# Opening loads reordered, the norm gains spread by a matmul, and three instead of five head groups transposed on TensorE

## The chip, the cores and the metric

One core of one Trainium2 chip. The time is device microseconds of a whole run of the kernel; the runs of one kernel lie 1 to 3 us apart, so a difference is read from the interval given with it. "PE" is TensorE, "PEld" its loading of weights, "ACT" ScalarE, "DVE" VectorE, "POOL" GpSimd, "SP" the queue of SyncE, which here only issues DMAs. PEclk is the granted share of the TensorE clock. A trace is one profiled run; its times count from the start of the span.

## The reference, cut to what matters

```python
# q, k, v: (8, 12, 448, 64); g_q, g_k: (64,)
q_n, k_n = rmsnorm(q, g_q), rmsnorm(k, g_k)
attn = softmax(q_n @ k_n.T / 8)          # per head
x = (attn @ v) -> (3584, 768)            # heads side by side
out = ((x @ w1) * (x @ w2)) @ w3 @ w_out # w1, w2: 768x1024; w3: 1024x1024; w_out: 1024x768
```

The kernel multiplies w3 and w_out once (w34 = w3 @ w_out) and then needs three products per token.

## The kernel before: the parts that matter here

The work is cut into 24 quads of 4 heads. Each quad has 4 slots; in slot t = 4 i + sl PE computes a quarter of quad i's scores, a part of quad i-1's P.V, and "fillers". In slots 1 to 13 the fillers are the w34 product: 8 transposes of w3 chunks and 16 product units. Quad n's normalised q and k are prepared some slots earlier and are needed transposed (qkT). For the first N_PE_T quads PE transposes them; for the others a DMA transpose, issued by SP, does it.

```python
    N_PE_T = 5
    LAG = 4
    SHIFT = [0, 0, 0, -1, -2, -3, -4]        # quad 1, 2, ...: slots earlier than PREP says
    PREP = {"load": -8, "sq0": -5, "red0": -5, "sq1": -4, "red1": -4, "alpha": -3,
            "sc0": -3, "t0": -2, "sc1": -2, "t1": -1}
    ...
        if pe:
            s["qks", pr] = qks               # prep_pe_transpose: 8 PE transposes and a DVE copy
        else:
            nc.sync.dma_start_transpose(
                out=s["qkT"][:, pr], in_=qks.rearrange("p t j h d -> p (t j h d)"))
    ...
        nc.gpsimd.dma_start(out=gq_b, in_=g_q.unsqueeze(0).broadcast_to([NP, D]))
        nc.gpsimd.dma_start(out=gk_b, in_=g_k.unsqueeze(0).broadcast_to([NP, D]))
        ...
        load_qk(0, split=2, k_eng=nc.scalar)   # q on SP, k on ACT's queue
        load_qk(1)                             # quad 2's load follows in slot 0
        nc.gpsimd.tensor_copy(out=gate, in_=st[0]["k"][:, HQ - 1, 0, 0:1])  # weights wait here
        load_wout(0, 0); load_wout(0, 1)       # half of w_out        (joined in one line here)
        for c in range(4):
            load_w3(c)
        load_v(0)
        load_wout(1, 0); load_wout(1, 1)       # the other half
        # in the slots: w3 4, 5, v 1, w3 6, 7, v 2, then 16 loads of w1/w2, then v 3
```

## Time and profile before

| | before |
|---|---|
| median of the first 3 runs | 391.38 us |
| span of the profiled run | 389.7 us |
| PE busy | 372.7 us (96%) |
| ACT, DVE busy | 285.1, 242.3 us |
| first w3 transpose on PE | 20.45 us |

PE is the bound. The row of granted clock of the page has 40 slices of 9.7 us, in tenths:

```profile
PEclk9579999999999999999999999999999999999999
```

The 5 and the 7 are the second and third slice, 9.7 to 29 us. Everything after is full speed.

### The profile page before, as it was taken

The page shows a single profiled execution, that of the slowest core. Times are in us where ns is not written, and L with a number is a line of the kernel's source. Part 1 is how long each engine was busy: PE and PEld are TensorE (multiplying, and loading weights), DVE is VectorE, ACT ScalarE, POOL GpSimd, SP SyncE. Part 2 cuts the span into 40 slices and gives each one's busy share as a digit, 9 for nine tenths or more (in the row PEclk, how much of TensorE's full clock was granted, in tenths as well). Part 3 has the DMA queues.
Part 4 walks back from the last instruction along what each step waited for, and adds up shares of the span by engine and source line. Part 5 has one row for each costly group of instructions (what it writes and reads, how often), then busy time and mean ns, then how long its engine had stood idle before and what let it go on. Part 6 is the DMA issues. An engine that isn't in the chain of part 4 may idle for free.

```text
span 389.7 us, 14802 instructions
## 1 busy us (share of the span) xinstructions
PE 372.7 (96%) x6688; PEld 193.4 (50%) x6688; DVE 242.3 (62%) x383; ACT 285.1 (73%) x467; POOL 35.3 (9%) x61
## 2 busy tenths in 40 slices
PE   5489999999999999999999999999999999999995
PEld 1154554544544455445544554445445555456563
DVE  1776766887767577567766766757776672234232
ACT  4469889998888885897899768888889857751210
POOL 5332530000000000000000000000000000000000
PEclk9579999999999999999999999999999999999999
DMA  8999998376994479575878489659855651003014
GB/s 196 221 236 239 221 229 172 64 153 142 208 200 87 113 159 226 119 161 98 188 172 155 83 210 206 84 109 212 197 87 122 121 140 26 3 12 114 2 26 140
DMA packets 78367, 55.08 MB, mean 141 GB/s; under 512 B 37824, under 2 KB 72160, under 8 KB 78304
## 3 DMA queue, kind: packets, MB, share of 16 engines
q1 hardware_dynamic: 61568, 41.30, 44.4%
q0 software_dynamic: 16256, 12.38, 22.0%
q8 instruction: 52, 0.85, 1.0%
q10 hardware_dynamic: 480, 0.46, 0.4%
q14 instruction: 11, 0.09, 0.1%
HBM read 46.72 MB, written 11.01 MB: 148 GB/s over the span
## 4 chain that ended last, share of the span: by engine, by line
PE 88%; DMA 4%; ACT 3%; DVE 2%; POOL 0%; issue 0%; ACTq 0%
PE pa L314 19%; PE po L314 19%; PE pb L314 19%; PE pv L259 15%; PE sc L235 12%; PE wps L301 4%; DMA w3s<-in_moe_w_dram 3%; DMA k_sb<-in_k_dram 1%; PE w3T_ps L293 1%; ACT P L244 1%; ACT sq L157 1%; ACT w34s L286 1%; PE qkT_ps L220 1%; DVE qtmp L188 1%; DVE qks L201 0%; POOL w_outs L140 0%
## 5 line engine op out<-in xcount | busy, mean ns | idle before, releaser
L244 ACT ACTIVATE P<-sc 112x896 bf16<-112x896 f32 x192 | 165.3, 915 | 42.1 <-PE sc L235 42.1
L344 DVE TENSOR_TENSOR abT<-pb,a_sb 128x448 bf16<-128x448 f32 x64 | 40.0, 625 | 77.1 <-PE pb L314 56.7
L314 PE MATMUL pa<-xT,w1s 128*32 128x448 bf16 x1536 | 84.0, 353 | 0.0
L314 PE MATMUL pb<-xT,w2s 128*32 128x448 bf16 x1536 | 83.8, 352 | 0.0
L314 PE MATMUL po<-w34s,abT 128*32 128x384 bf16 x1792 | 78.0, 326 | 0.0
L166 DVE TENSOR_REDUCE ssq<-sq 112x16 f32<-112x1024 f32 x48 | 58.3, 1215 | 13.9 <-ACT sq L157 13.9
L314 PEld LDWEIGHTS <-abT 128*32 128x32 bf16 x1792 | 47.4, 97 | 27.6 <-issue 2.4
L235 PE MATMUL sc<-qkT 64*112 64x448 bf16 x384 | 57.4, 378 | 0.7 <-DVE qkT L223 0.7
L314 PEld LDWEIGHTS <-w2s 128*32 128x32 bf16 x1536 | 41.2, 97 | 31.3
L314 PEld LDWEIGHTS <-w1s 128*32 128x32 bf16 x1536 | 39.8, 96 | 34.0 <-issue 4.7
L331 ACT CAST a_sb<-pa 128x448 bf16<-128x448 f32 x64 | 33.9, 530 | 26.5 <-PE pa L314 26.5
L363 DVE COPY o_sb<-po 128x384 f32<-128x384 f32 x56 | 31.2, 557 | 31.5 <-PE po L314 31.5
L259 PE MATMUL pv<-P,v_sb 112*32 112x448 bf16 x768 | 45.1, 355 | 0.0
L120 POOL DMA_DIRECT2D v_sb<-in_v_dram x24 | 17.0, 708 | 238.8 <-PE pv L259 217.6
L188 DVE TENSOR_TENSOR qtmp<-q_sb,alpha 112x512 bf16<-112x512 f32 x48 | 32.8, 683 | 6.1 <-ACT alpha L177 6.1
L235 PEld LDWEIGHTS <-qkT 64*112 64x112 bf16 x384 | 17.4, 126 | 31.8 <-issue 29.1
L201 DVE TENSOR_TENSOR qks<-k_sb,alpha 112x512 bf16<-112x512 f32 x48 | 32.9, 684 | 0.0
L157 ACT ACTIVATE sq<-q_sb 112x512 f32<-112x512 f32 x48 | 30.4, 634 | 1.6 <-DMA q_sb<-in_q_dram 1.6
L275 DVE TENSOR_TENSOR xT<-pv,r 128x448 bf16<-128x448 f32 x48 | 29.6, 617 | 3.2 <-PE pv L259 3.2
L157 ACT ACTIVATE sq<-k_sb 112x512 f32<-112x512 f32 x48 | 30.0, 625 | 0.0
L259 PEld LDWEIGHTS <-v_sb 112*32 112x32 bf16 x768 | 16.2, 95 | 23.7 <-issue 15.2
L301 PE MATMUL wps<-w_outs,w3T 128*128 128x384 bf16 x128 | 23.7, 335 | 0.0
(36 smaller groups left out, 174.4 us busy)
## 6 DMA issues: line engine op xcount, KB each, us to landing
q_sb<-in_q_dram SPq DMA_DIRECT2D x23, 448.0 KB, 5.5
k_sb<-in_k_dram SPq DMA_DIRECT2D x23, 448.0 KB, 6.1
v_sb<-in_v_dram POOLq DMA_DIRECT2D x24, 224.0 KB, 4.6
out_dram<-o_sb SPq DMA_DIRECT2D x8, 336.0 KB, 3.8
out_dram<-o_sb SPq DMA_DIRECT2D x8, 288.0 KB, 3.3
w3s<-in_moe_w_dram POOLq DMA_DIRECT2D x8, 256.0 KB, 15.1
out_dram<-o_sb SPq DMA_DIRECT2D x8, 240.0 KB, 4.3
w_outs<-in_moe_w_out_dram POOLq DMA_DIRECT2D x4, 384.0 KB, 13.4
```

The costliest lines, as they stand in the source:

```text
L157: nc.scalar.activation(out=sq[:, t], in_=src[:, hs], func=AF.Square)
L166: nc.vector.tensor_reduce(out=s["ssq"][:, :, hs, :], in_=s.pop(("sq", pr)), axis=AX, op=ADD)
L188: nc.vector.tensor_tensor(out=qtmp.transpose([0, 2, 1, 3]), in0=s["q"][:, hs], in1=alpha[:, 0, hs].unsqueeze(3).broadcast_to([NP, 2, J, D] ...
L201: nc.vector.tensor_tensor(out=qks[:, 1].transpose([0, 2, 1, 3]), in0=s["k"][:, hs], in1=alpha[:, 1, hs].unsqueeze(3).broadcast_to([NP, 2, ...
L235: nc.tensor.matmul(out=sc[:, u, 0:S], lhsT=qkT[u * D : (u + 1) * D, pr, J + jk, :], rhs=qkT[u * D : (u + 1) * D, pr, 0:J, :].rearrange("d ...
L244: nc.scalar.activation(out=P[:, 2 * pr : 2 * pr + 2, jk, :], in_=sc[:, :, 0:S], func=AF.Exp)
L259: nc.tensor.matmul(out=ps[h * HALF : (h + 1) * HALF, :], lhsT=w, rhs=P[:, h, jk, :], start=(jk == 0), stop=(jk == J - 1), tile_position=(0 ...
L301: nc.tensor.matmul(out=ps[:, 0:NH], lhsT=w3T[:, gc, fc * 128 : (fc + 1) * 128], rhs=w_outs[:, gc, nh * NH : (nh + 1) * NH], start=(gc == 0 ...
L314: nc.tensor.matmul(out=ps[32 * h : 32 * h + 32, 0:n], lhsT=lhsT[:, 32 * h : 32 * h + 32], rhs=rhs, start=start, stop=stop, tile_position=( ...
L331: nc.scalar.copy(out=a_sb, in_=ps[:, 0:S])
L344: nc.vector.tensor_tensor(out=abT[bp][:, fi, odd * S : (odd + 1) * S], in0=ps[:, 0:S], in1=a_tiles.pop((b, fi)), op=MULT,)
L363: nc.vector.tensor_copy(out=o_sb[:, nh * NH : (nh + 1) * NH], in_=ps[:, 0:NH])
```

## The change

Its intent: get w3's chunks to PE sooner (they gate the w34 product), get the weights going sooner, take the two gains off the weight queue, and take transposes off PE.

```diff
-    N_PE_T = 5
+    N_PE_T = 3
-    LAG = 4
+    LAG = 8
+    LOADS_0 = ["o0", "w0", "w1", "w2", "v0", "w3", "w4"]   # o: half of w_out, w: w3 chunk
+    LOADS_1 = ["w5", "v1", "w6", "w7", "o1", "v2"]
+    GATE = ("q", 0)
...
-        nc.gpsimd.dma_start(out=gq_b, in_=g_q.unsqueeze(0).broadcast_to([NP, D]))
-        nc.gpsimd.dma_start(out=gk_b, in_=g_k.unsqueeze(0).broadcast_to([NP, D]))
+        nc.scalar.dma_start(out=g_row[:, 0], in_=g_q.unsqueeze(0))
+        nc.scalar.dma_start(out=g_row[:, 1], in_=g_k.unsqueeze(0))
...
-        nc.gpsimd.tensor_copy(out=gate, in_=st[0]["k"][:, HQ - 1, 0, 0:1])
+        nc.gpsimd.tensor_copy(out=gate, in_=st[0][GATE[0]][:, GATE[1], 0, 0:1])
...
-                nc.vector.tensor_tensor(out=gq_b, in0=gq_b, in1=gk_b, op=MULT)
-                nc.vector.tensor_scalar(out=g_b, in0=gq_b, scalar1=8.0, ..., op0=MULT)
+                nc.vector.scalar_tensor_tensor(out=gp_row, in0=g_row[:, 0], scalar=8.0,
+                                               in1=g_row[:, 1], op0=MULT, op1=MULT)
+                nc.tensor.matmul(out=g_ps, lhsT=ones_row, rhs=gp_row, start=True, stop=True)
+                nc.vector.tensor_copy(out=g_b, in_=g_ps)
```

LAG = 8 puts all the product units that need the second half of w_out behind those that need the first.

More of the change, by code (lines that the diff above doesn't have):

```diff
@@ L59 @@
     big_pool = ctx.enter_context(tc.tile_pool(name="big", bufs=2))
-    N_PE_T = 5
+    N_PE_T = 3
     N_SQ_ACT = 24
     W34_EV = "DA"
-    LAG = 4
+    LAG = 8
+    LOADS_0 = ["o0", "w0", "w1", "w2", "v0", "w3", "w4"]
+    LOADS_1 = ["w5", "v1", "w6", "w7", "o1", "v2"]
+    GATE = ("q", 0)
+    QK1_AT = -1
     SHIFT = [0, 0, 0, -1, -2, -3, -4]
@@ L81 @@
     w3T = big_pool.tile([128, CF, DFF], BF, tag="big", name="w3T")
-    gq_b = const.tile([NP, D], FP, name="gq_b")
-    gk_b = const.tile([NP, D], FP, name="gk_b")
+    g_row = const.tile([1, 2, D], FP, name="g_row")
+    gp_row = const.tile([1, D], BF, name="gp_row")
+    ones_row = const.tile([1, NP], BF, name="ones_row")
     g_b = const.tile([NP, D], BF, name="g_b")
@@ L145, in load_wout, with load_any @@
         )
+    def load_any(x):
+        kind, a = x[0], int(x[1])
+        if kind == "o":
+            load_wout(a, 0)
+            load_wout(a, 1)
+        elif kind == "w":
+            load_w3(a)
+        else:
+            load_v(a)
     def prep_sq(i, pr, on_act=False):
@@ L405 @@
         nc.vector.memset(ones, 1.0)
+        nc.vector.memset(ones_row, 1.0)
         load_qk(0, split=2, k_eng=nc.scalar)
+        nc.scalar.dma_start(out=g_row[:, 0], in_=g_q.unsqueeze(0))
+        nc.scalar.dma_start(out=g_row[:, 1], in_=g_k.unsqueeze(0))
         nc.scalar.preload_act_table_set("natural_log_exp_and_others")
-        load_qk(1)
+        if QK1_AT < 0:
+            load_qk(1)
         make_identity(nc, ident)
-        nc.gpsimd.tensor_copy(out=gate, in_=st[0]["k"][:, HQ - 1, 0, 0:1])
-        load_wout(0, 0)
-        load_wout(0, 1)
-        for c in range(4):
-            load_w3(c)
-        load_v(0)
-        load_wout(1, 0)
-        load_wout(1, 1)
+        nc.gpsimd.tensor_copy(out=gate, in_=st[0][GATE[0]][:, GATE[1], 0, 0:1])
+        for x in LOADS_0:
+            load_any(x)
         warm(16)
@@ L423 @@
             if pr == 0:
-                nc.vector.tensor_tensor(out=gq_b, in0=gq_b, in1=gk_b, op=MULT)
-                nc.vector.tensor_scalar(
-                    out=g_b, in0=gq_b, scalar1=8.0, scalar2=None, op0=MULT
-                )
+                nc.vector.scalar_tensor_tensor(
+                    out=gp_row, in0=g_row[:, 0], scalar=8.0, in1=g_row[:, 1],
+                    op0=MULT, op1=MULT,
+                )
+                g_ps = mm_psum.tile([NP, D], FP, tag="mm", name="g_ps")
+                nc.tensor.matmul(
+                    out=g_ps, lhsT=ones_row, rhs=gp_row, start=True, stop=True
+                )
+                nc.vector.tensor_copy(out=g_b, in_=g_ps)
             prep_scale(0, pr, pe=True)
@@ L430 @@
                 prep_pe_transpose(0, 0)
-        wq = [lambda c=c: load_w3(c) for c in range(4, CF)]
-        wq.insert(2, lambda: load_v(1))
-        wq.append(lambda: load_v(2))
+        wq = [lambda x=x: load_any(x) for x in LOADS_1]
         for h in range(HQ):
@@ L475 @@
                 t = 4 * i + sl
+                if t == QK1_AT:
+                    load_qk(1)
                 mine = agenda.pop(t, [])
```

## The prediction

> **What bounds the kernel now.** I read the busy table per stretch first, then the chain that ended last, then the timeline and transfers of the opening. The table, cut at three borders (columns: stretch, length, busy time and instruction count of PE, PEld, DVE, ACT, POOL, then granted clock, DMA share, GB/s):
>
> ```profile
> 0.00:25.00 25.00, 13.95 (x66) 6.43 (x67) 11.60 (x20) 11.40 (x21) 10.31 (x22) 0.73 1.06 217
> 25.00:68.00 43.00, 41.71 (x427) 22.78 (x425) 30.79 (x49) 38.73 (x67) 13.10 (x22) 1.00 1.11 217
> 68.00:385.00 317.00, 317.00 (x6200) 164.18 (x6196) 199.38 (x315) 234.93 (x381) 11.93 (x17) 1.00 0.59 125
> ```
>
> From 68 us to 385 us PE has no gap, and the diff touches nothing there but a few early transposes. So the end moves by as much as PE's progress at 68 us moves. All that can be won lies in 0 to 25 us (11 us of idle PE, and a mean clock of 0.73) and in the 1.3 us of gaps from 25 to 68 us. The chain in order of time (start us, length us, what) says what holds the opening:
>
> ```profile
> 1.19 5.17 DMA k_sb<-in_k_dram
> 6.36 0.05 issue
> 6.42 0.18 POOL gate L410
> 6.60 1.48 POOL w_outs L140 x2
> 8.07 12.33 DMA w3s<-in_moe_w_dram
> 20.41 0.05 issue
> 20.45 1.05 PE w3T_ps L293 x8
> ```
>
> The first chunk of w3 lands at 20.41 us, PE's first w3 transpose starts at 20.45 us, and from there PE hardly stops. That landing is the bound of the opening. The 2.9 us which VectorE loses to the two gains are not on this path:
>
> ```profile
> 10.15 0.22 DVE L424 TENSOR_TENSOR gq_b<-gq_b,gk_b 112x64 f32<-112x64 f32 x1 [3.10 <-DMA gk_b<-in_g_k_dram]
> 10.52 0.68 DVE L188 TENSOR_TENSOR qtmp<-q_sb,alpha 112x512 bf16<-112x512 f32 x1
> 16.00 0.31 SPq L109 DMA_DIRECT2D q_sb<-in_q_dram  x1
> ```
>
> In the first line VectorE sits idle 3.10 us for g_k. Its next useful work, the scaling at 10.52 us, could have begun at 7.63 us, where alpha ends. The third line is the q load of quad 3, which waits until quad 0's scaling has freed its buffer.
>
> The transfers: q/k of quads 0 to 2 fill queue 1 first. The DMA view of 5 to 12 us, then of 19 to 27 us (queue: packets, MB, share):
>
> ```profile
> q1 hardware_dynamic: 1512, 1.49, 85.7%
> q0 software_dynamic: 64, 0.06, 16.9%
> ...
> q0 software_dynamic: 1010, 1.04, 75.9%
> q1 hardware_dynamic: 907, 0.91, 40.5%
> ```
>
> The weights (queue 0) are issued from 6.54 us, but until 12 us that queue moves only the 0.06 MB of the gain broadcasts; its first weight packet starts at 12.2 us. Later the two queues share by packets, nearly 1:1.
>
> **What the Trainium skill says.** "DMA: Bandwidth & Descriptors", section "Issuing engines are not separate DMA queues": transfers from any engine run on the same 16 DMA engines and interleave. The trace agrees: the DMA line reads 9 throughout from 6 us, so an earlier start of one load is a later end of another. Same page, "Queues, rings and completion order": a DMA engine goes round-robin over the queues it has work for, by packets. The 1010 to 907 packets above agree. "TensorE: Matmul & The Clock Gate", "Part 1: The HAM clock gate": idle for about 3.4 us brings half clock, as much sustained work brings it back. The trace agrees roughly: the warm-up ends at 6.45 us, the clock is 0.50 from about 11.7 us, and back at 1.00 at 25.0 us, 4.5 us after the w3 transposes began. Same page, "Part 4: PE-mode transpose": the result goes to PSUM, so a VectorE copy follows; that copy is 0.62 us here.
>
> **The change part by part.**
>
> Gains as one row. Removed: two broadcast loads (2 x 28 KB) from the weight queue, and 0.42 us of VectorE. Added: two one-row loads on ACT's queue behind k (that queue's last k lands near 6.4 us, so the row by about 7 us), one small VectorE operation, one matmul with 64 columns, and one PSUM copy, together about 0.7 us by estimate. The reduction ends at 7.04 us, so qtmp starts at about 7.8 instead of 10.52 us: quad 0 is ready 2.5 to 3 us earlier. None of that reaches the end, because PE then waits longer for w3. It has a price instead: quad 0's buffers come free at about 13.2 instead of 16.0 us, so quad 3's q and k (0.92 MB) are issued then. Their first packets followed 3 us after issue before (16.0 to 19.0 us), so they join at about 16.2 us, while w_out and w3 are still under way.
>
> Gate on the first q. That half lands at 4.62 us against 6.36 us for the last k, so the weights are issued 1.7 us earlier, and their first packet moves from 12.2 to at best 10.5 us. Queue 1 then still has 0.35 MB + 1.6 us x 0.22 MB/us = 0.70 MB left. Sharing packet by packet (768 B of w_out against 1024 B of q/k), queue 0 has moved 0.53 MB when queue 1 has drained; with 0.245 and 0.205 MB/us as the rates of each alone, that takes 2.9 + 2.6 = 5.5 us, so until 16 us. Before, queue 0 had also moved 0.53 MB by 16 us (12 to 16 us view). So the early gate buys nothing for w3: the wires were full, only the order changed.
>
> Order of the loads. The first three (w_out half, 0.79 MB; w3 chunk 0, 0.26 MB) keep their places, so nothing moves here for the first transpose. From 16.2 us queue 0 now shares with quad 3: the last 0.26 MB of w_out and the 0.26 MB of chunk 0 give away about 0.3 MB, that is some 1.2 us, against 0.3 us given away before; minus 0.2 us for the removed broadcasts. First w3 landing: **later by 0.8 us** (0 to 1.5). Moving the other half of w_out back brings w3 chunks 4 to 7 earlier by up to 5 us, but PE waited for none of those after 25 us, so it is worth nothing. LAG = 8 makes the second-half products come last, as that order needs; the counts per slot are the same.
>
> Three quads on PE instead of five. Quads 3 and 4 lose 32 PE transposes. The timeline shows what one set of 8 occupies:
>
> ```profile
> 53.93 0.56 PE L220 MATMUL qkT_ps<-ident,qks 112*128 112x112 bf16 x8
> 54.42 0.58 PE L235 MATMUL sc<-qkT 64*112 64x448 bf16 x4
> ```
>
> From start to start 0.4 to 0.5 us, so 4 sets are 1.6 us, and quad 4's sets also cost 0.6 us of waiting for qks (67.2 to 67.8 us). Saved on the path: **2.2 us**. Given back: quad 3's set 0 now travels by DMA. Its qks is done at about 52.8 us and its scores start at 58.0 us. Before, such transfers landed thus, on a half-empty DMA:
>
> ```profile
> DMA to landing us min/median/max: 2.9/4.3/6.7
> ```
>
> At 53 us the DMA is still full of w1/w2/v. A transpose is 896 packets of 256 B, 56 per engine; alternating with 2048 B weight packets of 172 ns each it would move slowly until these end, about 56 to 58 us. I expect landing at 57 to 61 us. Also, in SP's order quad 5's q and k now stand between quad 3's two transposes. They are issued near 54 us, not 41 us, and set 1 lands behind 0.92 MB at about 65 us, just when it is needed (65.3 us). Stall of PE: 0 to 3 us, **1.4 us taken**.
>
> Sum: + 0.8 (w3 later) + 0.2 (cold clock a little longer) - 2.2 + 1.4 = + 0.2 us. I shade this by 1.3 us, since the stall needs single-packet alternation, for which this trace has no example with transposes, and since the other parts are all aimed the right way: **390.3 us**.
>
> **The rivals.** (1) The weights really come earlier: if their late start is a delay of 5.6 us from issue rather than a full DMA, and quad 3's load starts late enough, chunk 0 lands 1 to 2 us sooner and the time is 387 to 388 us. For: 12.2 us follows 6.54 us with no weight packet between. Against: total bytes ahead of chunk 0 are the same. (2) The DMA transposes become the bound at slots 12 and 14: 393 to 395 us. For: a DMA at over 100% share there. Against: they are only 0.46 MB, and need about 1.2 us each when alone. (3) The clock: quad 0's earlier work could shorten or shift the cold stretch; its length can differ by a 3.4 us window, at half clock 1.7 us of work.
>
> **Range and chances.** The parts have about 1, 1 and 1.5 us of doubt, together 2 to 2.5 us: 387.3 to 393.3 us. 2% is 7.8 us; the opening would have to deliver w3 near 12 us for that, or stall twice as long as the worst I see. Faster 0.04, same 0.94, slower 0.02.
>
> **What would show it.** qtmp's first start near 7.8 us; first weight packet near 10.5 us; quad 3's q load issued near 13 us; first w3 transpose at 20.5 to 22 us; 6 copies of qkT from PSUM, not 10; and PE idle at quad 3's scores, ended by a DMA. The prediction is wrong if the first w3 transpose starts before 19.5 us, or if PE waits over 3 us for a qkT.

## The result, and the profile after

| | before | after |
|---|---|---|
| median, runs of the same rounds (4 each) | 391.58 us | 396.25 us |
| lowest to highest | 390.85 to 392.08 | 395.76 to 396.57 |
| ratio after / before | | 1.012 (95%: 1.010 to 1.0139) |

The kernel is 1.2% slower, 4.7 us: within 2%, but above the predicted range (387.3 to 393.3 us).

The table per stretch, after, with the borders of the prediction's table and one more at 100 us (columns: stretch, length, busy time and count of PE, PEld, DVE, ACT, POOL, granted clock, DMA share, GB/s):

```profile
0.00:25.00 25.00, 15.27 (x90) 7.34 (x91) 13.84 (x25) 12.92 (x23) 9.20 (x21) 0.80 1.05 225
25.00:68.00 43.00, 37.84 (x347) 19.20 (x344) 22.84 (x35) 32.89 (x59) 12.28 (x21) 0.92 1.10 200
68.00:100.00 32.00, 30.55 (x544) 14.86 (x540) 25.78 (x40) 29.94 (x51) 2.10 (x3) 1.00 0.77 146
100.00:385.00 285.00, 285.00 (x5588) 146.95 (x5584) 175.52 (x278) 209.61 (x336) 10.53 (x15) 1.00 0.67 125
```

Before 25 us PE has done more (90 matmuls, not 66) at a better clock. Between 25 and 68 us it was busy for 3.9 us less (37.84 us, not 41.71; 347 matmuls, not 427), and at a lower clock. From 100 us it is full again, as before. So the opening was a gain, and the loss lies between 25 and 75 us. The chain that ended last shows both (start us, length us, what):

```profile
4.62 0.05 issue
4.68 0.18 POOL gate L427
4.86 1.55 POOL w_outs L145 x2
6.41 11.88 DMA w3s<-in_moe_w_dram
18.29 0.05 issue
18.34 1.05 PE w3T_ps L308 x8
...
48.78 1.47 PE wps L316 x9
50.26 9.51 DMA qkT<-qks
59.76 0.04 issue
59.81 0.99 PE sc L250 x3
60.80 1.62 PE pv L274 x15
62.42 4.44 PE wps L316 x16
```

The first six lines answer to those of before: the first w3 transpose comes at 18.34 us, 2.1 us earlier. The line at 50.26 us is new: quad 3's first DMA transpose is issued then, and PE's scores wait for it until 59.8 us. The line at 62.42 us: 16 matmuls of the product (two units of 8) take 4.44 us there; 16 of them took 2.7 us before. The waits of PE in the first 100 us, largest first (total, times, longest):

```profile
PE sc L250 <- DMA qkT<-qks: 5.1, 1, 5.1
...
PE sc L250 <- ACT P L259: 1.4, 2, 1.0
```

And what SP did meanwhile, and how long its transposes took over the whole run:

```profile
50.26 1.32 SPq L225 DMA_TRANSPOSE qkT<-qks  x1
51.67 1.25 SPq L114 DMA_DIRECT2D q_sb<-in_q_dram  x1
53.02 0.68 SPq L114 DMA_DIRECT2D k_sb<-in_k_dram  x1
...
DMA to landing us min/median/max: 3.0/4.0/11.3
```

The longest before was 6.7 us. Of the loads that quad 5 needs, issued at 51.67 and 53.02 us, the kernel before had issued its q at 41.24 us; they are behind the transpose now in the order in which SP issues. (That delay turned out to cost nothing; see e5.)

### The profile page after: what moved, and what is told of

Its sections match the earlier page's. It is cut to its first block, busy times and chain, and to the rows that moved or that the text cites. A ratio compares the mean times of both kernels' runs of the same rounds, so it can differ in the third digit from the quotient of the medians.

```text
span 394.5 us, 14750 instructions
## 1 busy us (share of the span) xinstructions
PE 373.3 (95%) x6657; PEld 191.1 (48%) x6657; DVE 240.2 (61%) x380; ACT 285.3 (72%) x467; POOL 34.1 (9%) x59
## 4 chain that ended last, share of the span: by engine, by line
PE 88%; DMA 6%; ACT 3%; DVE 1%; POOL 0%; issue 0%
PE pa L329 19%; PE po L329 19%; PE pb L329 18%; PE pv L274 15%; PE sc L250 12%; PE wps L316 4%; DMA w3s<-in_moe_w_dram 3%; DMA qkT<-qks 2%; ACT P L259 1%; DMA q_sb<-in_q_dram 1%; PE w3T_ps L308 1%; ACT sq L172 1%; POOL w_outs L145 0%; ACT w34s L301 0%; DVE ssq L181 0%; PE qkT_ps L235 0%
## 5 line engine op out<-in xcount | busy, mean ns | idle before, releaser
L250 PE MATMUL sc<-qkT 64*112 64x448 bf16 x384 | 58.3, 381 | 7.3 <-DMA qkT<-qks 5.1
L316 PE MATMUL wps<-w_outs,w3T 128*128 128x384 bf16 x128 | 24.8, 346 | 0.0
```

Of the source, the lines that this page charges most:

```text
L250: nc.tensor.matmul(out=sc[:, u, 0:S], lhsT=qkT[u * D : (u + 1) * D, pr, J + jk, :], rhs=qkT[u * D : (u + 1) * D, pr, 0:J, :].rearrange("d ...
L316: nc.tensor.matmul(out=ps[:, 0:NH], lhsT=w3T[:, gc, fc * 128 : (fc + 1) * 128], rhs=w_outs[:, gc, nh * NH : (nh + 1) * NH], start=(gc == 0 ...
```

## The experiments

Every run below gave correct results. All times are medians, with the ratio to the kernel before of the same rounds; the four at the end (e13 to e16) are single runs. I give "the first w3 transpose" from each trace.

### Which part makes the loss: e1, e2, e8

The changed kernel with quads 3 and 4 back on PE:

```diff
-    N_PE_T = 3
+    N_PE_T = 5
```

> The changed kernel with quads 3 and 4 transposed on PE again. Theory 1 (the late DMA transpose of quad 3 and the half clock behind it are the whole loss, the opening is a gain): first w3 transpose near 18.3 us as in the changed kernel, no PE wait for a DMA at slot 12, time 389.3 us (388.5 to 390.2). Rival (the earlier opening is lost again later by itself, e.g. ACT or w1/w2 become the bound): 391 us or more.

Measured: 390.36 us, ratio 0.9955 (0.9931 to 0.998). No PE wait after 25 us up to 60 us. So everything else in the change is a gain of 1.8 us (0.0045 x 391.7), a little less than I expected: the median is 0.2 us outside my range.

The kernel before with only the transposes changed (N_PE_T = 5 to 3):

> The kernel before with quads 3 and 4 transposed by DMA, nothing else. Theory 1: PE waits 4 to 6 us for quad 3's first transpose, the clock falls to half, time 396 to 399 us. Rival (the stall comes from the new order of the loads, which puts the weight traffic on top of the transpose): PE waits under 2 us, time 390 to 392.5 us.

Measured: 399.24 us, ratio 1.0185 (1.0157 to 1.0213). PE waits 5.0 us for the transpose, and the clock falls behind it:

```profile
PE sc L235 <- DMA qkT<-qks: 5.0, 1, 5.0
...
62.00:69.00 7.00, 6.71 (x35) 2.81 (x36) 0.00 (x0) 3.33 (x5) 0.00 (x0) 0.54 0.85 159
```

The rival (the new order of the loads makes the stall) is out: the stall is there with the old order.

The changed kernel with only quad 4 and later on the DMA transpose (N_PE_T = 3 to 4):

> The changed kernel with only quad 4 (not 3) on the DMA transpose. Theory 1 (only quad 3's transposes meet the full DMA): no PE wait for a DMA, and 1.4 us of PE time saved against five quads on PE: 388.6 to 390 us. Rival (any transpose before the weights are done stalls PE): 392 us or more.

Measured: 389.17 us, ratio 0.994 (0.9915 to 0.9965). Quad 3 alone costs 1.012 - 0.994, 1.8% or 7.1 us. The cause sits in one quad. That quad 4 on the DMA is a gain is not shown: e8 and e1 differ by 1.2 us between the medians, but their intervals overlap, and the traces place the difference in the opening (first w3 transpose at 17.89 us in e8, 19.54 in e1). From quad 3's first scores to the first product with w1, the stretch that holds quad 4's transposes, PE needs 10.56 us in e1 (56.89 to 67.45) and 10.51 us in e8 (54.98 to 65.49). Without the transposes PE waits there for ACT's exponentials, 1.4 us in two waits, as it does in the changed kernel.

### Why quad 3's transpose costs more than its wait: e5

Dummy matmuls where PE would stand still:

```diff
+                if t == 12:
+                    warm(20)
                 if i < NQ:
                     qk_exp(i, sl)
```

> The changed kernel with 20 dummy matmuls on PE just ahead of quad 3's scores, where PE waits for the DMA transpose (about 4.3 us of work inside a 5.1 us wait; their result is not used). Theory 1a (the wait costs twice: its own 5 us, and about 3 us because PE comes out of it at half clock for 6 us): the wait for the transpose still ends near 59.8 us, the clock stays 1.00, time 392.5 to 394.2 us. Rival (the half clock is hidden behind other waits): 395.7 to 397 us.

Measured: 393.71 us, ratio 1.0058 (1.0029 to 1.0087). The scores still started at 59.7 us, and quad 5's q was issued at 51.45 us, as late as in the changed kernel. The stretch of the stall and the one behind it, in the changed kernel:

```profile
54.70:59.80 5.10, 0.01 (x1) 0.00 (x0) 1.22 (x1) 1.77 (x4) 0.00 (x0) 0.93 1.32 186
59.80:67.00 7.20, 7.19 (x38) 2.97 (x40) 0.00 (x0) 3.44 (x6) 0.00 (x0) 0.58 0.81 163
```

and with the dummies:

```profile
54.70:59.80 5.10, 4.20 (x21) 1.77 (x21) 1.22 (x1) 1.54 (x4) 0.00 (x0) 1.00 1.34 187
59.80:67.00 7.20, 7.20 (x68) 3.28 (x68) 2.07 (x4) 5.95 (x11) 0.00 (x0) 1.00 0.77 161
```

Behind the stall PE was equally busy in both, but at clock 0.58 it got through 38 matmuls, at 1.00 through 68. The dummies compute nothing that is used, and give back 1.012 - 1.0058, that is 2.4 us. The first product with w1, in the changed kernel, with the dummies, and in e8:

```profile
73.20 1.32 PE L329 MATMUL pa<-xT,w1s 128*32 128x448 bf16 x24
70.21 1.32 PE L329 MATMUL pa<-xT,w1s 128*32 128x448 bf16 x24
65.49 1.32 PE L329 MATMUL pa<-xT,w1s 128*32 128x448 bf16 x24
```

Counted from quad 3's first scores (59.81, 59.70, 54.98 us) that is 13.39, 10.51 and 10.51 us. So with the clock kept up nothing is left of the loss behind the stall; in particular the late loads of quad 5 cost nothing. The wait is paid twice: 5.1 us of standing, and 2.4 us (by the ratios) to 2.9 us (by these traces) of coming out cold, that is at half clock.

### Why the transpose is slow: e6, e7

The changed kernel with v of quad 3 and later held back until quad 3's scores are out, so that the weight queue is empty sooner:

```diff
-        wq.append(lambda: load_v(3))
...
+                if t == 12:
+                    nc.gpsimd.tensor_copy(out=gate, in_=st[3]["P"][:, 0, 0, 0:1])
+                    load_v(3)
```

> The changed kernel with the loads of v for quad 3 and later held until quad 3's first scores are out (a POOL copy of one column of P ahead of them). Theory 1b (quad 3's transpose is slow because its 256 B packets alternate with the weight queue's packets): its second half no longer meets v packets and takes 0.6 instead of 2.3 us; it lands near 58 us, not 59.8; the wait falls to about 3.3 us; time 391.5 to 394.5 us, the lower end if the shorter wait no longer drops the clock. Rival (the transpose is slow by itself or by its issue): lands at 59.5 us or later, time 396 us.

Measured: 392.68 us, ratio 1.0019 (0.9994 to 1.0043). The wait fell to 2.3 us, more than I had expected. The transpose's packets took from 54.5 to 57.0 us; in the changed kernel from 54.2 to 59.1 us. It met little other traffic (139 packets of the weight queue from 54 to 57 us), but the clock fell all the same:

```profile
59.80:67.00 7.20, 7.20 (x56) 3.26 (x57) 2.47 (x5) 4.77 (x11) 1.97 (x3) 0.84 0.95 134
```

The third number from the end is the clock, 0.84 (0.58 in the changed kernel). Cut finer, PE resumed at 57.67 us at full clock, 1.00 until 58.7 us, and then had 0.50 from 58.75 to 62.1 us; in the changed kernel it has 0.50 from 59.1 to 65.8 us. What the two queues carried in the changed kernel from 54 to 59 us:

```profile
DMA packets 1966, 0.92 MB, mean 184 GB/s; under 512 B 961, under 2 KB 1868, under 8 KB 1966
q0 software_dynamic: 997, 0.64, 87.2%
q1 hardware_dynamic: 969, 0.28, 43.6%
```

The transpose is 896 packets of 256 B on q1. In these 5 us it got about one packet for each of the weight queue's, 969 to 997. By the first line, what it met was mostly packets of 512 B to under 2 KB (907; v's rows are 512 B), and only 98 larger ones.

The second test of the same theory was a cure that failed: prepare quads 3 and 4 two slots earlier (and quads 5 and 6 one).

```diff
-    SHIFT = [0, 0, 0, -1, -2, -3, -4]
+    SHIFT = [0, 0, -2, -3, -3, -4, -4]
```

> The changed kernel with the preparation of quads 3 and 4 moved two slots earlier (of quads 5 and 6 one or none), so that quad 3's transposes are issued near 40 us. Theory 1 (the lead of two slots is too short while the weights are being loaded): no PE wait for a DMA, the clock stays 1.00 after 25 us, time 387.5 to 389.5 us. Rival (the transposes stop something else, or ACT and VectorE pay for the earlier preparation): 391 us or more.

Measured: 396.75 us (394.19 to 400.46; the longest was a slow run and is not in the ratio), ratio 1.0107 (1.0073 to 1.0141). My expectation was wrong. The transpose was issued at 45.6 us, into denser weight traffic. From 49 to 58 us the queues carried:

```profile
q0 software_dynamic: 959, 1.45, 94.2%
q1 hardware_dynamic: 915, 0.23, 21.9%
```

Again nearly one to one, but the weight queue's packets are larger (1.45 MB in 959, against 0.64 MB in 997), so the same 896 small packets took 8.4 us. In e8, where quad 4's transpose meets no weights (63 to 65 us):

```profile
q1 hardware_dynamic: 951, 0.25, 74.3%
```

it took 1.3 us. So 1.3, 2.5, 4.9 and 8.4 us of packets for the same transfer, in the order of the traffic beside it. That this traffic makes the transpose slow is shown by e6 and e8; that the two queues alternate by packets is an explanation that fits the counts. It doesn't cover all of the delay: from issue to first packet the transpose took 3.9 us in the changed kernel (50.26 to 54.17 us), 3.6 us in e6, 4.0 us in e7, but 1.3 us in e8 (62.01 to 63.26 us). Until 54.1 us queue 1 moved nothing in the changed kernel, and the weight queue was full. What holds the start back stays open. And in e7 the delay had another victim: DVE stood 4.4 us because its buffer was still being read by the transpose.

```profile
59.59 0.42 DVE L210 TENSOR_TENSOR qks<-qtmp,g_b 112x512 bf16<-112x512 bf16 x1 [4.37 <-DMA qkT<-qks]
```

More lead does not help when the lead reaches back into denser traffic; fewer transposes under that traffic do (e8).

### Where the opening's gain comes from: e3, e4, e10

The gains as one row, nothing else:

> The kernel before with only the gains as one row (matmul spread). Theory A (the two broadcast loads slow the shared DMA engines and put some of them behind): w3 chunk 0 lands 1 to 2 us earlier (18.5 to 19.5 us), time 389.5 to 390.6 us. Rival B (the earlier gate is what brings w3 forward; VectorE was never on the path): w3 chunk 0 stays at 20 to 20.5 us, time 391 to 392 us.

Measured: 391.23 us, ratio 0.9985 (0.996 to 1.001). The first w3 transpose came at 17.95 us, 2.5 us earlier, but the time did not follow. With the gate on the first q added:

> The kernel before with the one-row gains and the gate on the first q. Theory A (bytes are conserved, the gate only reorders): within 0.4 us of the run with the one-row gains alone. Rival B (gate): 1 to 2 us faster than that run, first w3 transpose near 18.3 us, time 389 to 389.8 us.

Measured: 391.47 us, ratio 0.9998 (0.997 to 1.0025). The first w3 transpose at 18.24 us, and no gain at all. The trace says where it went, from 25 to 40 us:

```profile
PE w3T_ps L294 <- DMA w3s<-in_moe_w_dram: 2.0, 1, 2.0
```

(L294 is the w3 transpose in that kernel.) PE, 2.2 us ahead, ran into the chunk of w3 that stands behind the second half of w_out in the old order, at 31.4 us, and stood there for 2.0 us. (In e3 it was 1.0 us.) Only the new order:

```diff
-        for c in range(4):
-            load_w3(c)
-        load_v(0)
-        load_wout(1, 0)
-        load_wout(1, 1)
+        # w3 0, 1, 2, v 0, w3 3, 4; later w3 5, v 1, w3 6, 7, both parts of w_out, v 2
-    LAG = 4
+    LAG = 8
```

> The kernel before with only the new order of the loads and LAG = 8. Theory (chunk 0 keeps its place, so w3's first transpose stays near 20.4 us; the order pays only once chunk 0 is early and chunk 3 becomes the next wait): 391 to 391.8 us. Rival (the order alone gives the opening's gain): 390.3 us or less.

Measured: 390.83 us, ratio 0.9972 (0.9946 to 0.9997): first w3 transpose at 20.48 us as before, and yet some 1.1 us faster, between my two expectations. It has no PE wait between 25 and 60 us. The kernel before had one there, and I had read it wrongly:

```profile
34.21 0.62 PE L293 MATMUL w3T_ps<-ident,w3s 128*128 128x128 bf16 x8 [0.62 <-ACT sq L157]
34.21 0.45 PEld L293 LDWEIGHTS <-w3s 128*128 128x128 bf16 x8 [1.06 <-DMA w3s<-in_moe_w_dram]
```

The first line puts PE's 0.62 us down to ACT's squares, which w3's transpose does not read. The trace's landing records have chunk 4 of w3 at 34.17 us, and the weight load on PE (PEld) at the same 34.21 us is put down to a w3 load. It was the DMA. So the order removes a wait that exists before, and a larger one that the other two parts would create. The intervals of e1, e3, e4 and e10 overlap one another, so the times alone don't rank these parts; as one opening (e1) they are 1.8 us.

### What moves the first chunk: e9, e13 to e16

Is it the removed broadcasts, or the side effect that two more loads on the hardware queues delay quad 2's q and k from 2.71 to 5.0 us? The gains' rows from POOL's queue:

```diff
-        nc.scalar.dma_start(out=g_row[:, 0], in_=g_q.unsqueeze(0))   # and g_k
+        nc.gpsimd.dma_start(out=g_row[:, 0], in_=g_q.unsqueeze(0))   # and g_k
```

> The kernel before with the gains as one row each, but loaded from POOL's queue, where the broadcasts were, so that quad 2's q and k are issued as early as before (2.7 us). Theory A (the broadcast packets of up to 1.5 us themselves hold up the DMA engines and leave them uneven): w3 chunk 0 lands at 18 to 19 us as with the rows on ACT's queue. Rival (it is the later issue of quad 2's q and k, 5.0 us in place of 2.7, that lets the weights through): chunk 0 at 20 us or later. Time 390.5 to 391.8 us either way.

Measured: 391.23 us, ratio 0.9983 (0.9952 to 1.0014), first w3 transpose at 19.49 us: between the two. The opposite test, broadcasts kept and two unused one-row loads on ACT's queue:

> The kernel before, broadcasts kept, with two extra one-row loads on ACT's queue behind k into a tile that nothing reads. Theory L (the two loads on a hardware queue delay quad 2's q and k to 5.0 us and that lets the weights through): quad 2's q is issued near 5 us and the first w3 transpose starts at 18 to 19 us. Theory A (the broadcasts hold the engines up): quad 2's q is issued near 5 us, yet the first w3 transpose stays at 20 to 20.6 us. 19.2 to 19.8 us: both, about half each.

> The one-row gains from POOL's queue once more (first look: 19.49 us). Theory A: the first w3 transpose at 18 to 19 us. Theory L: at 20 us or later. Both parts: 19.2 to 19.8 us again.

> The one-row gains on ACT's queue once more, for the spread: the first w3 transpose at 17.9 to 19.2 us (first look 17.95 us).

> The kernel before once more, for the spread of its first w3 transpose: 20.3 to 20.7 us (first look 20.45 us; two other kernels with the broadcasts 20.55 and 20.48 us).

Measured, first w3 transpose: e13 20.11 us (quad 2's q was issued at 5.04 us, as meant; one run, 391.60 us), e14 19.53 us (391.32 us), e15 19.55 us (391.26 us), e16 19.62 us (391.23 us). e13 is what theory A says, e14 repeats e9. The plain repeats e15 and e16 both missed what I expected of them: the same kernel's first w3 transpose moves by 0.8 us (before: 20.45 and 19.62) and 1.6 us (gains' rows: 17.95 and 19.55) from trace to trace. Taken together:

| kernels | traces | first w3 transpose, mean (lowest to highest) |
|---|---|---|
| broadcasts, gate on k (before, e2, e10, e13, e16) | 5 | 20.24 us (19.62 to 20.55) |
| one-row gains, gate on k (e3, e9, e14, e15) | 4 | 19.13 us (17.95 to 19.55) |
| one-row gains, gate on the first q (after, e1, e4 to e8, e12) | 8 | 18.51 us (17.89 to 19.54) |

The later issue of quad 2 does not do it by itself (e13). The one-row gains bring about 1.1 us, the gate about 0.6 us; with this spread neither share is more than a tendency, their sum, 1.7 us, is clear of it. The mechanism behind the 1.1 us is not shown: the broadcast packets last up to 1.6 us in the first trace, which fits.

### Can the opening go further: e11, e12

The best version so far (four quads on PE) with two load buffers instead of three, so that quad 2's q and k come behind the first weights:

```diff
-    load_pool = ctx.enter_context(tc.tile_pool(name="load", bufs=3))
+    load_pool = ctx.enter_context(tc.tile_pool(name="load", bufs=2))
```

> The changed kernel with four quads on PE and two, not three, load buffers for q and k, so that quad 2's q and k (0.92 MB) are issued only when quad 0's buffers are free, near 14 us, behind w_out and w3's first chunks. Theory (chunk 0 waits for the bytes ahead of it): chunk 0 lands 1.5 to 3 us earlier, near 16 us, and the time falls to 386.8 to 388.6 us. Rival (the later loads of every quad then stall the squares on ACT): 389.5 us or more, with ACT waiting for q.

Measured: 391.97 us, ratio 1.0005 (0.998 to 1.0031). The opening did as expected: first w3 transpose at 16.17 us. The rival took it back later, from 20 to 110 us:

```profile
ACT sq L172 <- DMA k_sb<-in_k_dram: 2.0, 2, 1.9
```

ACT waits for a late k, PE for ACT, and from 60 to 70 us the clock has a mean of 0.83.

Four quads on PE with 16 dummy matmuls in the idle stretches of the opening:

```diff
+                warm_mm(5)          # behind the gains' copy
...
                 if t == 0:
+                    warm_mm(6)
                     prep_pe_transpose(0, 1)
+                if t == 1:
+                    warm_mm(5)
```

> The changed kernel with four quads on PE and 16 dummy matmuls in PE's idle stretches of the opening (5 after the gain matmul, 6 ahead of quad 0's second transposes, 5 ahead of the first w3 transpose). Theory (the opening's half clock, 11.4 to 21.7 us, costs PE up to 1.9 us behind the first w3 transpose): the clock stays 1.00 or comes back earlier, 387.5 to 388.7 us. Rival (PE is then held by chunks 1 and 2 of w3 and by quad 1's preparation): 389 us, no gain.

Measured: 389.02 us, ratio 0.9927 (0.9902 to 0.9953). The clock was indeed 1.00 from 11 to 25 us, where e8 has 0.63:

```profile
11.00:25.00 14.00, 9.60 (x78) 4.92 (x80) 10.34 (x16) 9.53 (x17) 3.62 (x6) 1.00 1.19 238
```

and the time is that of e8 (389.17 us) within the noise. PE, now fast, waits instead: 0.53 us for w3's second chunk and 0.75 us for DVE's normalised q. So its next transposes start at 22.49 us, against 22.64 us in e8. The opening's half clock was hidden behind the loads and DVE's preparation, as the rival said. Both e8 and e12 beat the kernel before, by 0.6 and 0.7%.

## Why the prediction was wrong, point by point

**Right.** The bound was read correctly: from about 75 us PE is full in both kernels, so all is decided earlier. qtmp starts at 8.59 us (said 7.8), the first weight packet at 10.75 us (said at best 10.5), quad 3's q is issued at 13.9 us (said 13). Rival 2, "the DMA transposes become the bound at slots 12 and 14: 393 to 395 us", is what happened, at slot 12 alone, and somewhat beyond its numbers. The reason given, small packets beside the weight queue's, is borne out by e6 and e7 for the time of the packets. Both signs that the prediction named for being wrong came about: the first w3 transpose before 19.5 us (18.34), and a wait over 3 us for a qkT (5.1).

**The term that failed: "Stall of PE: 0 to 3 us, 1.4 us taken".** It was mis-sized in two ways. First, the transfer. I let it land 4 to 8 us after its issue (57 to 61 us for 52.8 us). It took 9.5 us, and 9.4 us in e2 (issued 52.88, scores at 62.3 us): 3.9 us passed before its first packet, and its 896 packets took 4.9 us, beside mostly v's 512 B packets and not the 2048 B ones that I had named. The wait was 5.1 us. Second, the consequence. I quoted the clock's rule and used it for the opening, but did not apply it to my own stall. The gap of 5.1 us was followed by a mean clock of 0.58 for the next 7.2 us, and e5 puts 2.4 to 2.9 us on that. So the term was 7.5 to 8.0 us, not 1.4 us. Quad 3 in all cost 7.1 us (e8 against the changed kernel). The 1.3 us by which I shaded the sum towards faster rested on the doubt about the packets, and was the wrong way round. The range was 3 us each way, wider than the doubt of 2 to 2.5 us that the text adds up, and still too narrow.

**A second term that was too large: "Saved on the path: 2.2 us".** Of this, 1.4 us were quad 4's: half of the 1.6 us of transposes, and 0.6 us of waiting. In the traces they are not saved: PE waits 1.4 us for ACT's exponentials in that stretch instead (e8 against e1, 10.51 and 10.56 us). What is left is quad 3's share, about 0.8 us by the prediction's own figure.

**The step with the wrong sign: "First w3 landing: later by 0.8 us".** It came 1.7 us earlier (mean of 8 against 5 traces; and 1.2 - 0.3 - 0.2 gives 0.7, not 0.8). I had argued that the bytes ahead of chunk 0 stay the same, so that "the early gate buys nothing for w3". Total bytes do not say when one chunk is complete. By the time chunk 0 landed the weight queue had moved 1400 KB before (56 of them the broadcasts) but 1100 KB after, by the trace's packets, though half of w_out and the chunk itself are 1024 KB. That some of the 16 engines were ahead of others would explain it, but the trace does not tell them apart. My 0.2 us for the removed broadcasts was too small, if the 1.1 us of the table above is theirs. Which property of the broadcasts does it stays open.

**The reading that failed: "PE waited for none of those after 25 us, so it is worth nothing".** This was about chunks 4 to 7 of w3. The 0.62 us wait at 33.6 us was such a wait under another name (ACT), and without the new order the earlier start would have run into 1 to 2 us more of it (e3, e4). The order made about 1.1 us alone (e10).

Together, from the two traces: PE was ready for quad 3's scores 3.3 us earlier than before (59.81 - 5.09 = 54.72, not 58.04 us), waited 5.1 us, and then took 2.8 us longer to the first product with w1 (13.39 us, not 10.57), where it starts at 73.20, not 68.61 us. That is + 4.6 us, and the spans differ by 4.8 us. (The ratios of e1, e8 and the changed kernel also sum to the result, but they do so by construction.)

## What to carry to other kernels

Ask of a transfer not only how many bytes but in how many packets, and beside what: the 896 small packets here took 1.3 us alone and 4.9 to 8.4 us beside another full queue, and starting them earlier was no cure, because that queue's packets were larger then (e7). When PE stalls, look at the granted clock behind the stall: here 5.1 us of waiting cost 2.4 to 2.9 us more, and even 2.3 us (e6) were followed by half clock. And when a first wait is shortened, look for the next one before counting the gain, in the same stream of loads (e4) and on other engines (ACT in e8); a wait that the profile puts down to an engine which the instruction does not read may be a hidden DMA, as in the kernel before at 34.2 us.

## What the Trainium skill lacked or had wrong

- "DMA: Bandwidth & Descriptors", "Queues, rings and completion order", gives the round-robin by packets, and the counts of the runs agree (969 to 997 packets; 915 to 959). No page gives what a DMA transpose costs beside other loads: one of 224 KB took 1.3 us of packets alone and 4.9 to 8.4 us beside the weight queue's, and its first packet came 3.9 us after its issue there, 1.3 us alone.
- "TensorE: Matmul & The Clock Gate", "Why this matters for your kernels", advises no idle gaps above about 3 us. That was not enough here: in e6 a wait of 2.3 us, ended at 57.67 us, was followed by a clock of 0.50 from 58.75 to 62.1 us, and in e11 the clock had a mean of 0.83 from 60 to 70 us with no single gap above 1.0 us.
- No page gives a cost for loading a 256 B row to 112 partitions as a broadcast beside other loads: the two loads' 32 packets of 1792 B lasted up to 1.6 us each here, and kernels without them had w3's first transpose about 1.1 us earlier (means of 4 and 5 traces; the mechanism is open).
